# Attention and expert layers on one core: keys loaded by head pairs, and the last tile scaled in two halves

## The chip, the cores and the metric

The kernel runs on one core of a Trainium2 chip. Its engines are TensorE (PE in the rows; PEld is its weight load), VectorE (DVE), ScalarE (ACT), GpSimd (POOL) and SyncE (SP), which here issues most transfers between HBM and SBUF (on-chip memory). Matrix products go to PSUM. The metric is the device time of one execution in microseconds (us), as the median of several runs.

## The reference

Attention in a window, then a layer of eight experts of which each token takes one, all in float32:

```python
batch, n_heads, seq, head_dim = (8, 8, 576, 64)
scores = scale * np.matmul(q, k.transpose(0, 1, 3, 2))
mask = (rel >= 0) & (rel < window)                      # window = 128
scores = np.where(mask, scores + bias[None], -1000000000.0)
attn = np.exp(scores - np.max(scores, axis=-1, keepdims=True))
attn = attn / (np.sum(attn, axis=-1, keepdims=True) + 1e-09)
x = np.matmul(attn, v)          # as (B*S, H*D) = (4608, 512)

logits = x @ w_gate             # eight experts
expert_idx = np.argmax(logits, axis=1)
# gate_w: the chosen expert's softmax value
h = np.maximum(xe @ w1[e], 0.0) # 512 -> 1024, for the tokens of expert e
out[mask] = gate_w[mask, None] * (h @ w2[e])   # 1024 -> 512
```

## The kernel before

**Attention in chunks.** 36 chunks of 128 queries each, all eight heads (four head pairs; a pair's two heads lie in the two halves of the 128 partitions). A batch has 576 queries: four chunks m = 0 to 3, and a rest of 64. The rests of an even and the following odd batch share one *tail* chunk, which stands between the two: batch 0 has chunks 0 to 3, chunk 4 is the tail of batches 0 and 1, batch 1 has chunks 5 to 8, and so on. So an odd batch is first used in a tail chunk (13 for batch 3, 22 for batch 5, 31 for batch 7), an even one in its chunk m = 0 (9 for batch 2, 18 for batch 4, 27 for batch 6). A query sees the 128 keys up to its own, so chunk m reads columns 128(m - 1) to 128(m + 1) of the keys, and a tail chunk columns 384 to 576.

**Order of the work.** The table `WHEN` places each operation of a chunk in the order of program, in units of a chunk: S0 and S1 (`scores`, line 161) compute the scores of head pairs 0 and 1, and of 2 and 3; then come the maximum, the exponentials, the transposes, the products with the values and so on, up to four chunks later. Each engine runs its own instructions in the order in which the program has them, and waits at semaphores for the others. In `scores`, matmuls of a bias (line 173) come first, then 16 products of queries and keys (line 182) in four rounds of four: the first pair of the two for subblocks 0 to 3 and both heads, then the second pair. In the trace each of the 16 has two rows. In a tail chunk subblocks 0 and 1 are of the even batch, 2 and 3 of the odd one, so that the odd batch's second pair is in the last quarter.

**Loads of keys.** `batch[b]` is a tile `k_sb` of 128 partitions x 4 pairs x 576 columns, two of them in turn. `load_k(b, i)` (line 59) loads piece i. For batches 0 and 1 calls stand in the opening; for batches 2 to 7 a step (a quarter of a chunk) has them, counted from the batch's first chunk `ch` (line 273):

```python
ahead.setdefault(4 * ch + KA + KD * p, []).append((load_k, b, p))   # KA = -16, KD = 4
```

So pieces 0 to 3 are issued 16, 12, 8 and 4 steps before the batch's first chunk in the order of program. SP, which issues them, also has the queries, the values, the expert weights and the writes of finished rows in its queue, in the order of program. A piece is a range of columns of all four pairs, `KEYS = ((0, 128), (128, 256), (256, 384), (384, S))`; an odd batch begins with the last range.

**Expert layers.** From about 220 us on, TensorE runs eight experts one after another. In `layer2` (line 931) the last product of a tile (f == 7) is followed by a multiplication with the gate, from PSUM to SBUF: ScalarE has the even tiles, VectorE the odd ones (lines 944 to 947). Then GpSimd scatters the rows to `out` (`put`, line 926). The last expert has 462 places: four tiles, the last (t = 3) with 78 rows. A similar pair is in `narrow` (lines 919 to 922), where ScalarE scales one group of rows of a tile and VectorE the next.

Of the kernel before, what the change touches and what calls it, by code (L numbers as in the profile page):

```python
# [14 lines left out]
AF = mybir.ActivationFunctionType  # L15
ALU = mybir.AluOpType
# [5 lines left out]
N, DM, E, F = B * S, H * D, 8, 1024  # L22
# [14 lines left out]
def attention(ctx, tc, st, qT, qE, kT, v, c1, cb, iw, load_c2, logits, chunk_done, chunks, begun):  # L37
    nc = tc.nc
# [12 lines left out]
    batch = {}  # L51
# [7 lines left out]
    def load_k(b, i, gate=False):  # L59
        if b not in batch:  # L60
            batch[b] = qkv.tile([128, NP, S], F32, name="k_sb", bufs=2)
        c, d = KEYS[(i - b % 2) % 4]
        x = batch[b][:, :, c:d]
        if gate:
            hold(x[:, 0, 0:1])
        nc.sync.dma_start(out=x, in_=kT[b][:, :, c:d])

    def hold(x):
        keep(tc, nc.vector.memset(x, 0.0))
# [68 lines left out]
    for p in (0, 2):  # L138
        nc.vector.tensor_scalar(out=q0[:, p:p + 2], in0=q0[:, p:p + 2], scalar1=0.125, scalar2=1.0, op0=ALU.mult, op1=ALU.mult)
    load_q(0, 1)  # L140
    load_k(0, 1)
    load_c2(0, 128)

# [4 lines left out]
    for n, (f, b, m) in dict(q2=(load_q, 0, 2), k2=(load_k, 0, 2), q3=(load_q, 0, 3), k3=(load_k, 0, 3), q4=(load_q, 0, 4),  # L148
                             r4=(load_q, 1, 4), k4=(load_k, 1, 0), r0=(load_q, 1, 0), k5=(load_k, 1, 1), r1=(load_q, 1, 1),
                             k6=(load_k, 1, 2), k7=(load_k, 1, 3)).items():  # L150
        loads[n] = lambda gate, f=f, b=b, m=m: f(b, m, gate)
# [244 lines left out]
PROF = tuple(-(-c // 128) for c in CAPS)  # L396
# [17 lines left out]
KEYS = ((0, 128), (128, 256), (256, 384), (384, S))  # L414
# [384 lines left out]
def moe_static(ctx, tc, st, w12, out):  # L799
    nc = tc.nc  # L800
# [14 lines left out]
    ys = {}  # L815
# [7 lines left out]
    def column(p, t):  # L823
        return st["idx"][:, t:t + 1] if p == 0 else st["pidx"][:, p * TT + t:p * TT + t + 1]
# [101 lines left out]
    def put(**kw):  # L926
        ins = nc.gpsimd.indirect_dma_start(**kw).ins  # L927
        tc.declare_no_dep(ins, group="rows", reason="every token is in one slot: the rows are distinct")
        tc.add_to_no_dep_group("rows", ins)

    def layer2(p, f, wh, wl, hh, hl, tiles=None):
        for t in range(PROF[p] - (p in NARROW)) if tiles is None else tiles:
            if f == 0:
                ys[t] = ps_y[t > 1].tile([128, DM], F32, name=f"y{t}_ps")
            n = min(128, CAPS[p] - 128 * t)
            tl = slice(128 * t, 128 * t + n)
            gh, gl = h0[f] if p == 0 and t < 2 else (hh, hl)
            for k, (a, b) in enumerate(((gh, wh), (gh, wl), (gl, wh))):
                nc.tensor.matmul(out=ys[t][0:n], lhsT=a[:, tl], rhs=b[:, 512:1024],  # L939
                                 start=(f == 0 and k == 0), stop=(f == 7 and k == 2))  # L940
            if f == 7:
                y = yp.tile([128, DM], F32, name="y")
                gt = xs[p][2]
                if t % 2 == 0:
                    nc.scalar.activation(out=y[0:n], in_=ys[t][0:n], func=AF.Copy, scale=gt[0:n, t:t + 1])  # L945
                else:
                    nc.vector.tensor_scalar(out=y[0:n], in0=ys[t][0:n], scalar1=gt[0:n, t:t + 1], scalar2=None, op0=ALU.mult)
                put(
                    out=out[:, :], out_offset=bass.IndirectOffsetOnAxis(ap=column(p, t)[0:n], axis=0),
                    in_=y[0:n], in_offset=None, bounds_check=N - 1, oob_is_err=False,  # L950
                )
# [5 lines left out]
    for f in range(NE):  # L957
        layer2(0, f, *w0[f], None, None, (0, 1))
        if f == 1:
            order = order_experts(tc, st, bank())  # L960
            next(order)
        if f in PF:
            prep(0, 2 + PF.index(f))
        if f in OS:
            next(order, None)
# [4 lines left out]
    for p in range(E):  # L970
        if p in NARROW:
            load_narrow(p, 0)
        for f in range(8):
            cur = layer1(p, f)
            if p + 1 < E:
                t = f - (p + 1 >= BY_PARTS)
                if 0 <= t < PROF[p + 1]:
                    gather(p + 1, t, cur[2] if p + 1 >= BY_PARTS else None)
                for t in range(PROF[p + 1]):
                    if f == min(t + (PP if p else PP0), 7):  # L980
                        prep(p + 1, t)
            if 8 * p + f > 8 * E - LAST:
                held.append(pend)
            elif pend is not None:
                layer2(*pend, whole if pend[0] == 0 and pend[1] < NE else None)
                if pend[0] in NARROW and pend[1] in (3, 7):
                    narrow(pend[0], pend[1] // 4)
            if (p, f) == (1, 0):
                overflow_table(tc, st)
            if (p, f) == (E - 1, 1):  # L990
                keep(tc, nc.gpsimd.drain())
            pend = (p, f) + cur
    held.append(pend)
    for t in range(PROF[-1]):
        for x in held:
            layer2(*x, (t,))
# [344 lines left out]
```

## Time and profile before

| | |
|---|---|
| median of 3 runs | 644.63 us (644.35 to 645.72) |
| the profiled execution | 642.3 us, of which the span is 640.6 us |
| TensorE busy | 626.6 us, 98% of the span |
| its weight loads (beside it) | 536.9 us, 84% |
| VectorE / ScalarE / GpSimd busy | 380.9 / 316.4 / 294.5 us: 59%, 49%, 46% |
| mean granted TensorE clock | 0.996 of 2.4 GHz |
| transfers | 97.44 MB, mean 152 GB/s |

The span reaches from the first to the last instruction of the profiled execution; all times of rows count from its start. Busy shares are averages over stages: attention lies between 0 and some 220 us, the experts behind it. Matmuls are pipelined, so two that follow each other overlap in the rows. The time of a transfer "to landing" counts from its issue by SP to the last update of its semaphore.

### The profile page before, as it was taken

How to read it: one execution, taken by the hardware profiler on the slowest of the kernel's cores; microseconds unless marked ns; L12 is line 12 of the kernel's file. 1: busy time of each engine (PE TensorE's matmuls, PEld its weight loads, DVE VectorE, ACT ScalarE, POOL GpSimd, SP SyncE). 2: the span in 40 equal slices, each digit the busy share in tenths (PEclk: the TensorE clock that was granted, in tenths of full speed). 3: DMA queues.
4: the chain of work that ended last, by engine and by line, in shares of the span. 5: the costliest groups of instructions: out<-in, count | busy, mean ns of one | idle time of the engine just before them, and what ended most of it. 6: DMA issues, size and time to landing. Idle time of an engine off the chain costs nothing.

```text
span 640.6 us, 17972 instructions
## 1 busy us (share of the span) xinstructions
PE 626.6 (98%) x7125; PEld 536.9 (84%) x7125; DVE 380.9 (59%) x949; ACT 316.4 (49%) x963; POOL 294.5 (46%) x405
## 2 busy tenths in 40 slices
PE   7999999999999999999999999999999999999995
PEld 4788888878887888988988898898898888888884
DVE  4568877969888785536553654555456355455411
ACT  6878889888878314524342334334233333434311
POOL 2644656858646050067227607733750750670202
PEclk9999999999999999999999999999999999999998
DMA  8775996786743162374535325433442632543101
GB/s 249 237 228 156 293 277 192 216 289 190 220 143 86 51 189 81 144 251 112 185 123 165 106 77 184 117 100 134 143 118 86 196 113 70 183 128 125 65 1 61
DMA packets 60072, 97.44 MB, mean 152 GB/s; under 512 B 12293, under 2 KB 30597, under 8 KB 59986
## 3 DMA queue, kind: packets, MB, share of 16 engines
q1 hardware_dynamic: 51362, 76.25, 38.7%
q0 software_dynamic: 8336, 19.76, 10.7%
q8 instruction: 57, 0.93, 0.6%
q10 hardware_dynamic: 288, 0.26, 0.1%
q14 instruction: 29, 0.24, 0.1%
HBM read 77.27 MB, written 18.98 MB: 150 GB/s over the span
## 4 chain that ended last, share of the span: by engine, by line
PE 80%; issue 9%; POOL 4%; DVE 3%; ACT 1%; DMA 1%; SPq 0%; POOLq 0%; ACTq 0%; DVEq 0%
PE y_ps L939 25%; PE l_ps L734 24%; PE b_ps L240 9%; PE s_ps L182 5%; PE b_ps L209 5%; PE r_ps L248 5%; PE s_ps L173 2%; POOL xg L714 2%; PE s_ps L734 1%; POOL out L927 1%; ACT pe L201 1%; DMA c_sb<-c 1%; DVE nmax L195 1%; DVE s_ps L192 1%; PE x_ps L695 1%
## 5 line engine op out<-in xcount | busy, mean ns | idle before, releaser
L737 ACT ACTIVATE hh<-l_ps 128x320 fp32r<-128x320 f32 (+5 forms) x104 | 46.3, 446 | 199.2 <-PE l_ps L734 195.8
L741 DVE SCALAR_TENSOR_TENSOR hl<-l_ps,hh 128x320 fp32r<-128x320 f32 (+5 forms) x104 | 52.1, 501 | 147.0 <-ACT hh L737 146.8
L714 POOL DMA_INDIRECT xg<-xd,od_idx x112 | 116.5, 1040 | 34.5 <-issue 33.1
L201 ACT ACTIVATE pe<-s_ps,nmax 128x128 f32<-128x128 f32 x288 | 106.3, 388 | 31.7 <-DVE nmax L195 22.8
L939 PE MATMUL y_ps<-wh,hh 128*128 128x512 f32 (+5 forms) x280 | 110.3, 394 | 0.0
L939 PE MATMUL y_ps<-wl,hh 128*128 128x512 f32 (+5 forms) x280 | 109.8, 392 | 0.0
L939 PE MATMUL y_ps<-wh,hl 128*128 128x512 f32 (+5 forms) x280 | 109.7, 392 | 0.0
L927 POOL DMA_INDIRECT out<-y,od_pidx x33 | 34.6, 1049 | 150.0 <-ACT y L945 143.7
L224 POOL TENSOR_SCALAR_AFFINE_SELECT pT<-pT 128x512 f32<-128x512 f32 x112 | 71.4, 645 | 60.0 <-ACT pT L304 56.9
L1032 DVE TENSOR_TENSOR wl<-w_raw,wh 128x512 fp32r<-128x512 f32 x114 | 73.8, 689 | 33.2 <-ACT wh L1028 32.9
L734 PE MATMUL l_ps<-xh,wh 128*128 128x320 f32 (+8 forms) x416 | 81.2, 317 | 0.0
L734 PE MATMUL l_ps<-xl,wh 128*128 128x320 f32 (+8 forms) x416 | 80.6, 316 | 0.0
L734 PE MATMUL l_ps<-xh,wl 128*128 128x320 f32 (+8 forms) x416 | 80.4, 315 | 0.0
L734 PEld LDWEIGHTS l_ps<-xh,wh 128*128 128x128 f32 x416 | 67.8, 188 | 8.3 <-issue 1.2
L734 PEld LDWEIGHTS l_ps<-xl,wh 128*128 128x128 f32 x416 | 66.0, 188 | 2.0
L734 PEld LDWEIGHTS l_ps<-xh,wl 128*128 128x128 f32 x416 | 65.9, 188 | 2.0
L240 PE MATMUL b_ps<-pT,v_sb 128*64 128x128 f32 (+2 forms) x1152 | 66.3, 265 | 0.6 <-issue 0.6
L240 PEld LDWEIGHTS b_ps<-pT,v_sb 128*64 128x64 f32 (+1 forms) x1152 | 57.1, 136 | 9.7 <-issue 5.2
L201 ACT ACTIVATION_READ_ACCUMULATOR pe<-s_ps,nmax 128x1 f32 x288 | 64.5, 224 | 0.0
L939 PEld LDWEIGHTS y_ps<-wh,hl 128*128 128x128 f32 (+5 forms) x280 | 51.3, 183 | 13.2
L1028 ACT CAST wh<-w_raw 128x1024 fp32r<-128x1024 f32 x57 | 59.5, 1043 | 5.9 <-DMA w_raw<-w 5.9
L939 PEld LDWEIGHTS y_ps<-wl,hh 128*128 128x128 f32 (+5 forms) x280 | 51.3, 183 | 10.8
(216 smaller groups left out, 914.9 us busy)
## 6 DMA issues: line engine op xcount, KB each, us to landing
w_raw<-w SPq DMA_DIRECT2D x56, 512.0 KB, 3.6
xd<-x_sb SPq DMA_DIRECT2D x32, 258.0 KB, 4.1
v_sb<-v SPq DMA_DIRECT2D x32, 256.0 KB, 4.7
q_sb<-qT SPq DMA_DIRECT2D x31, 256.0 KB, 4.1
k_sb<-kT SPq DMA_DIRECT2D x23, 256.0 KB, 5.1
w_raw<-w SPq DMA_DIRECT2D x16, 256.0 KB, 4.5
k_sb<-kT SPq DMA_DIRECT2D x8, 384.0 KB, 4.5
w_n<-w SPq DMA_DIRECT2D x3, 1024.0 KB, 6.9
```

What stands on the lines that cost most here:

```text
L182: nc.tensor.matmul(out=s_ps[rows(u), c, n, x0:x1], lhsT=blocks["q", b, m][h, 2 * g + n, rows(u % 2 if tail else u)], rhs=batch[b][h, 2 * g ...
L201: nc.scalar.activation(out=pe[:, h, :], in_=s_ps[:, c, n, lo:lo + 128], func=AF.Exp, bias=nmax[:, 2 * c + n:2 * c + n + 1], scale=1.0, acc ...
L224: nc.gpsimd.affine_select(out=part(cut(kb)), in_=part(cut(1)), pattern=pat(sign), base=0, channel_multiplier=-sign, compare_op=op, fill=0.0)
L240: nc.tensor.matmul(out=x_ps[64 * c:64 * c + 64, p, q], lhsT=blocks["v", b, m - 1 + kb][0:kk, D * h:D * h + D], rhs=pT[0:kk, kb, h, q], sta ...
L714: ins = tc.nc.gpsimd.indirect_dma_start(out=g[:, s], out_offset=None, in_=parts, in_offset=bass.IndirectOffsetOnAxis(ap=idx[:, s], axis=0),)
L734: nc.tensor.matmul(out=ps, lhsT=a[:, 128 * d:128 * d + 128], rhs=b[:, d], start=(k == 0), stop=(k == 11))
L737: nc.scalar.activation(out=hh, in_=ps, func=AF.Relu)
L741: nc.vector.scalar_tensor_tensor(out=hl, in0=ps, scalar=0.0, in1=hh.bitcast(F32), op0=ALU.max, op1=ALU.subtract)
L927: ins = nc.gpsimd.indirect_dma_start(**kw).ins
L939: nc.tensor.matmul(out=ys[t][0:n], lhsT=a[:, tl], rhs=b[:, 512:1024], start=(f == 0 and k == 0), stop=(f == 7 and k == 2))
L1028: keep(tc, nc.scalar.copy(out=wh, in_=raw))
L1032: keep(tc, eng.tensor_tensor(out=wl[:, sl], in0=raw[:, sl], in1=wh.bitcast(F32)[:, sl], op=ALU.subtract))
```

## The change

For batches 2 to 7 a piece of keys is one head pair with all its 576 columns, in the order 0 to 3 for odd and even batches. The calls stay where they are. In the last tile of the last expert ScalarE scales the first 256 columns and VectorE the other 256; the other tiles are scaled as before.

```diff
     def load_k(b, i, gate=False):
         if b not in batch:
             batch[b] = qkv.tile([128, NP, S], F32, name="k_sb", bufs=2)
-        c, d = KEYS[(i - b % 2) % 4]
+        if b > 1:
+            nc.sync.dma_start(out=batch[b][:, i], in_=kT[b][:, i])
+            return
+        c, d = KEYS[(i - b) % 4]
         x = batch[b][:, :, c:d]
...
                 gt = xs[p][2]
-                if t % 2 == 0:
-                    nc.scalar.activation(out=y[0:n], in_=ys[t][0:n], func=AF.Copy, scale=gt[0:n, t:t + 1])
-                else:
-                    nc.vector.tensor_scalar(out=y[0:n], in0=ys[t][0:n], scalar1=gt[0:n, t:t + 1], scalar2=None, op0=ALU.mult)
+                half = DM // 2 if (p, t) == (E - 1, PROF[-1] - 1) else DM * (t % 2 == 0)
+                if half:
+                    nc.scalar.activation(out=y[0:n, 0:half], in_=ys[t][0:n, 0:half], func=AF.Copy, scale=gt[0:n, t:t + 1])
+                if half < DM:
+                    nc.vector.tensor_scalar(out=y[0:n, half:], in0=ys[t][0:n, half:], scalar1=gt[0:n, t:t + 1], scalar2=None, op0=ALU.mult)
                 put(
```

Line numbers move: the new loads stand in line 63, the score products in 185 (182 before), the scalings in 949 and 951 (945 and 947).

**SP, the third and fourth load of batch 5.** Its queue in chunks 20 and 21, with what each row waits for (DMAHW is a transfer's semaphore); `xd` are written rows, `w_raw` expert weights. Before:

```order
L66 DMA k_sb<-kT 128x4x128 [waits DMAHW1_49]
L1274 DMA xd<-x_sb_116 128x516 [waits DMAHW2_49,DVE_49]
L1017 DMA w_raw<-w 128x512 [waits DMAHW3_49,Activation_49,Pool_49]
L89 DMA v_sb<-v 128x512 [waits DMAHW4_49]
L80 DMA q_sb<-qT 128x512 [waits DMAHW5_49,PE_49,Pool_49]
L66 DMA k_sb<-kT 128x4x128 [waits DMAHW6_49]
```

Now:

```order
L63 DMA k_sb<-kT 128x576 [waits DMAHW1_49]
L1278 DMA xd<-x_sb_116 128x516 [waits DMAHW2_49,DVE_49]
L1021 DMA w_raw<-w 128x512 [waits DMAHW3_49,Activation_49,Pool_49]
L92 DMA v_sb<-v 128x512 [waits DMAHW4_49]
L83 DMA q_sb<-qT 128x512 [waits DMAHW5_49,PE_49,Pool_49]
L63 DMA k_sb<-kT 128x576 [waits DMAHW6_49]
```

The places and the waits are the same; only what the two loads bring has changed.

**TensorE, S1 of tail chunk 22, where batch 5 is first used.** `pT` and `v_sb` are operands of a product of an earlier chunk. Before:

```order
L173 LDWEIGHTS cb_sb
L173 MATMUL s_ps<-cb_sb 32x2x160
L182 MATMUL s_ps<-k_sb,q_sb 32x160 x16
L240 MATMUL b_ps<-pT,v_sb 64x128 [waits Activation_49,Pool_49]
L240 MATMUL b_ps<-pT,v_sb 64x128
L240 MATMUL b_ps<-pT,v_sb 64x128 [waits DMAHW3_49,Pool_49]
```

Now:

```order
L176 LDWEIGHTS cb_sb
L176 MATMUL s_ps<-cb_sb 32x2x160
L185 MATMUL s_ps<-k_sb,q_sb 32x160 x4
L185 MATMUL s_ps<-k_sb,q_sb 32x160 [waits DMAHW1_49]
L185 MATMUL s_ps<-k_sb,q_sb 32x160 x7
L185 MATMUL s_ps<-k_sb,q_sb 32x160 [waits DMAHW6_49]
L185 MATMUL s_ps<-k_sb,q_sb 32x160 x3
L243 MATMUL b_ps<-pT,v_sb 64x128 [waits Activation_49,Pool_49]
```

The 16 products waited for no load of their own before; now the fifth waits for pair 2 and the thirteenth for pair 3, the two loads shown above.

**VectorE, its last rows of the last expert.** `y` is the scaled tile. Before:

```order
L741 SCALAR_TENSOR_TENSOR hl_5127<-l_ps,hh_5126 128x462 [waits Activation_49]
L741 SCALAR_TENSOR_TENSOR hl_5129<-l_ps,hh_5128 128x462 [waits Activation_49]
L741 SCALAR_TENSOR_TENSOR hl_5125<-l_ps,hh_5124 128x462 [waits Activation_49]
L947 TENSOR_SCALAR y<-y_ps,gt 128x512 [waits DMASW3_49,PE_49]
L947 TENSOR_SCALAR y<-y_ps,gt 78x512 [waits DMASW5_49,PE_49]
```

Now:

```order
L744 SCALAR_TENSOR_TENSOR hl_5127<-l_ps,hh_5126 128x462 [waits Activation_49]
L744 SCALAR_TENSOR_TENSOR hl_5129<-l_ps,hh_5128 128x462 [waits Activation_49]
L744 SCALAR_TENSOR_TENSOR hl_5125<-l_ps,hh_5124 128x462 [waits Activation_49]
L951 TENSOR_SCALAR y<-y_ps,gt 128x512 [waits DMASW3_49,PE_49]
L951 TENSOR_SCALAR y<-y_ps,gt 78x256 [waits DMASW5_49,Activation_49]
```

The last row has half the columns, and it waits for ScalarE where it waited for TensorE.

## Rows read from the trace of the kernel before

**Rows 1.** The page's part 1: busy us (share of the span) xinstructions

```profile
PE 626.6 (98%) x7125; PEld 536.9 (84%) x7125; DVE 380.9 (59%) x949; ACT 316.4 (49%) x963; POOL 294.5 (46%) x405
```

**Rows 2.** Windows: us, busy of each engine (instructions), granted clock, DMA share, GB/s

```profile
30.00:125.00 95.00, 94.38 (x2237) 79.03 (x2243) 75.09 (x188) 80.15 (x335) 55.37 (x96) 1.00 0.77 225
125.00:220.00 95.00, 93.07 (x1982) 78.99 (x1967) 76.33 (x218) 70.77 (x290) 52.80 (x86) 1.00 0.59 177
```

**Rows 3.** Waits of PE, 30 to 230 us: total us, times, longest

```profile
PE s_ps L173 <- ACT pe L201: 0.7, 2, 0.4
PE s_ps L182 <- issue: 0.6, 1, 0.6
```

**Rows 4.** Transfers, 30 to 190 us: count, KB each, median us to landing

```profile
v_sb<-v SPq DMA_DIRECT2D x26, 256.0 KB, 4.9
q_sb<-qT SPq DMA_DIRECT2D x23, 256.0 KB, 4.1
k_sb<-kT SPq DMA_DIRECT2D x19, 256.0 KB, 5.2
```

**Rows 5.** Line 66 (loads of keys) over the span

```profile
DMA to landing us min/median/max: 3.3/4.7/7.6
```

**Rows 6.** SP's timeline, fourth loads of batches 3, 5, 6, 7: start, duration

```profile
71.36 0.55 SPq L66 DMA_DIRECT2D k_sb<-kT  x1
...
121.34 0.59 SPq L66 DMA_DIRECT2D k_sb<-kT  x1
...
147.99 0.55 SPq L66 DMA_DIRECT2D k_sb<-kT  x1
...
171.93 0.55 SPq L66 DMA_DIRECT2D k_sb<-kT  x1
```

**Rows 7.** Landings: keys of 71.36, 121.34, 147.99, 167.03; values of 120.34

```profile
DMA to landing us min/median/max: 3.9/3.9/3.9
...
DMA to landing us min/median/max: 7.6/7.6/7.6
...
DMA to landing us min/median/max: 3.8/3.8/3.8
...
DMA to landing us min/median/max: 4.7/4.7/4.7
...
v_sb<-v SPq DMA_DIRECT2D x1, 256.0 KB, 5.4
```

**Rows 8.** PE's timeline, S1 of chunks 13, 22, 27, 31: start, duration

```profile
74.65 0.73 PE L182 MATMUL s_ps<-k_sb,q_sb 64*32 64x160 f32 x32
...
124.93 0.73 PE L182 MATMUL s_ps<-k_sb,q_sb 64*32 64x160 f32 x32
...
154.44 0.64 PE L182 MATMUL s_ps<-k_sb,q_sb 64*32 64x32 f32 x32
...
176.18 0.73 PE L182 MATMUL s_ps<-k_sb,q_sb 64*32 64x160 f32 x32
```

**Rows 9.** Tile q_sb, 30 to 190 us, its products: ns min/median/max

```profile
L182 PE MATMUL s_ps<-k_sb,q_sb x1824: 186/296/321, 30.8 to 187.8; 64*32 64x160 f32 x141, 64*32 64x32 f32 x15, 64*32 64x96 f32 x11, 64*32 64x128 f32 x10
```

**Rows 10.** Timeline, end of the last expert, PE, DVE and ACT

```profile
633.39 0.40 PE L939 MATMUL y_ps<-wh,hl 128*78 128x512 f32 x1
...
633.83 0.75 DVE L947 TENSOR_SCALAR y<-y_ps,gt 78x512 f32<-78x512 f32 x1 [2.02 <-PE y_ps L939]
...
632.43 0.69 ACT L945 ACTIVATE y<-y_ps,gt 128x512 f32<-128x512 f32 x1 [1.85 <-PE y_ps L939]
```

**Rows 11.** Timeline, lines 920 and 922, ACT and DVE

```profile
274.44 0.46 ACT L920 ACTIVATE y<-y_ps,g_n 36x256 f32<-36x256 f32 x1
...
274.94 0.49 DVE L922 TENSOR_SCALAR y<-y_ps,g_n 36x256 f32<-36x256 f32 x1 [1.70 <-ACT y L920]
```

**Rows 12.** Windows at the end, columns as in rows 2

```profile
630.00:634.00 4.00, 3.79 (x17) 2.50 (x15) 0.93 (x2) 1.27 (x2) 2.53 (x3) 1.00 0.24 95
...
636.00:640.60 4.60, 0.00 (x0) 0.00 (x0) 0.00 (x0) 0.00 (x0) 0.00 (x0) 0.50 0.14 42
```


## Prediction

> **What bounds the kernel now.** I read the page first. TensorE is busy for 98% of the span [rows 1]; of the other engines none has over 59% (the table above). Then the windows, since attention (to about 220 us) and the expert layers have different limits: from 30 to 220 us, where the changed loads lie, TensorE works 187.45 of 190 us, at the granted clock 1.00 [rows 2]. Third, whom TensorE waited for there: 0.7 us on ScalarE in two waits, the rest "issue"; no row names a load [rows 3]. So TensorE is the bound, the keys are never late, and anything that makes TensorE wait is added to the end almost one to one. What it can give back behind 125 us is its idle time there, 95.00 - 93.07 = 1.93 us [rows 2].
>
> **The change, the keys.** For six batches (2 to 7), four loads of columns (128x4x128 or 128x4x192) become four loads of one head pair (128x576), at the same places of SP's queue: 24 loads, the same bytes, longer runs. Before, a chunk needed two of the four pieces and the other pieces only chunks later. Now a batch's first chunk needs all four: S0 reads pairs 0 and 1, S1 pairs 2 and 3. The pairs are issued 16, 12, 8 and 4 steps ahead, a chunk being four steps; the last has one chunk, and less where SP lags behind. The matmul that now waits stands in TensorE's own queue, and everything behind it waits with it.
>
> The pieces of before went out at the same places, so their issue times can be held against the first use of pair 3. The last load of batches 3, 5 and 7 left SP at 71.36, 121.34 and 171.93 [rows 6]. The S1 scores that will need it, in the tail chunks 13, 22 and 31, start at 74.65, 124.93 and 176.18 and take 0.73 [rows 8]; pair 3 of the odd batch is in the last of four equal rounds, and a matmul of these takes 0.30 [rows 9], so that round starts (0.73 - 0.30) = 0.43 in. From issue to need there are 3.7, 4.0 and 4.7 us. For the even batches the lead is longer; the shortest of the three is batch 6: issued 147.99 [rows 6], needed in a chunk that starts 154.44 [rows 8], 6.4 us against a landing of 3.8 [rows 7]. I cost these three at nothing, and pair 2 as well: it goes out a chunk earlier.
>
> Landing is the unknown. Key loads took 3.3 at least, 4.7 in the middle, 7.6 at most [rows 5]. The three loads in question, as pieces of 256 KB:
> - Batch 3: 3.9 [rows 7], so 0.2 late. Bounds: 0 (3.3) and 3.9 (7.6).
> - Batch 5: 7.6 [rows 7], the slowest of all, because four large transfers go out just ahead of it; the values issued 1.0 us earlier took 5.4 [rows 7]. Late by 7.6 - 4.0 = 3.6 at the same landing, by 1.4 at 5.4, by nothing at 3.3. I take the middle of the two nearest rows, 6.5: 2.5 us.
> - Batch 7: its landing isn't told; the key load before it took 4.7 [rows 7], so 0.0. Bounds 0 and 2.9.
>
> Stall together: 0.2 + 2.5 + 0.0 = 2.7 us (0 to 10.4).
>
> Do longer runs land sooner? A transfer of 288 KB is 1/8 more than 256 KB. Against it, queries and values of 256 KB, whose runs are 2,048 bytes, land in 4.1 and 4.9 us where key pieces take 5.2 [rows 4], 0.3 to 1.1 less; but they leave at other moments of the queue, so I leave the landings as they are and keep 1.1 for the range. The Trainium skill (DMA: Bandwidth & Descriptors, Specifications) asks for runs of at least 512 B for line rate. The old runs of 128 floats are exactly that; by this rule the longer runs buy no rate, the extra 32 KB costs a little, and the stall stays at 2.7 or grows. By the rows on queries and values batch 5's stall would be 1.4 instead of 2.5. No row isolates the run's length.
>
> **The change, the last tile.** Before: the last matmul runs 633.39 to 633.79, VectorE starts at 633.83 and takes 0.75 for 78x512 [rows 10], until 634.58; the scatter follows. Now ScalarE takes 256 columns and VectorE 256. In the new order VectorE's half waits for ScalarE (and not for TensorE), so it comes behind ScalarE's half. The trace has such a pair: ScalarE 0.46 for 36x256 at 274.44, then VectorE 0.49 at 274.94, 0.04 behind the other's end [rows 11]. 633.83 + 0.46 + 0.04 + 0.49 = 634.82, 0.24 us later than before. ScalarE is free: its previous tile ends at 632.43 + 0.69 = 633.12 [rows 10]. If the halves ran side by side it would be 0.75 - 0.49 = 0.26 less; those are the bounds.
>
> The Trainium skill (PSUM — Partial Sum Buffer, PSUM bank collisions raise a hardware error) says that two engines must not touch one bank in the same 32 partitions at once, readers and disjoint columns included. A tile of 512 float columns fills a bank, so by that rule two halves by columns can never overlap; the pair above agrees with it.
>
> **Sum.** 2.7 + 0.24, and of TensorE's 1.93 us of idle time behind chunk 22 I let 0.3 be given back (the waits on other engines are small [rows 3]): +2.6 us. The profiled execution took 642.3 us (span 640.6), which would become 644.9; it is 2.3 below the median of the runs shown, so I add to the median: 644.63 + 2.6 = 647.2.
>
> **Rivals.**
> - Landings in time. The 24 loads make fewer, longer runs and the queue ahead of batch 5's last pair drains sooner: landing 4.1, as the queries [rows 4], is 0.1 late; the other two 0.4 and 0. With the tail, and 0.3 given back, +0.4: 645.0. For it: the median of key loads is 4.7. Against: the DMA engines are loaded at 77% from 30 to 125 us [rows 2], and this one load took 7.6.
> - Faster. The freed transfer time removes idle time that TensorE has: two waits of 0.6 for "issue" stand among its waits (one shown in [rows 3]), and all its idle time from 30 to 220 us is 0.62 + 1.93 = 2.55 [rows 2]. Only if no pair is late and more than 1.55 of these 2.55 goes (1.3 and the tail's 0.24) does it decide; at 1.8 the time is 644.63 - 1.8 + 0.24 = 643.1. Against: none of it is a wait for a load.
> - The clock falls. A stall of about 3 us is longer than any idle time of TensorE in attention; the granted clock is 1.00 (2.4 GHz) up to 634 us and 0.50 (1.2 GHz) from 636 us, when the engine had nothing more to do [rows 12]. If the stall in chunk 22 lets it fall and it stays down for as long as is seen there, 4.6 us, half of that is lost: 647.2 + 2.3 = 649.5. The Trainium skill (TensorE: Matmul & The Clock Gate, Part 1) has the same two levels and says that activity lifts the lower one; the end of this trace agrees.
>
> **How the numbers follow.** The forecast (late pairs, 647.2) has a chance of 0.52, in time 0.28, the clock 0.10, faster 0.10. A measurement of this kernel can tell about 0.2%, 1.3 us. So slower 0.62, same 0.28, faster 0.10. The forecast's own range is 645.9 to 648.6 (batch 5 late by 1.4 to 3.6, the others by up to 0.4 more). The range reaches from the case in time and a part of the faster one to a part of the clock's: 643.9 to 650.0.
>
> **What would show it.** In the changed trace: a wait of TensorE on the scores' line for the keys' load, above all in chunk 22 near 125 us (2.5 us), hardly any in chunks 13 and 31, none in the even batches; VectorE's last row 78x256 starting 0.04 behind ScalarE's; the landing of 128x576 loads. If no row of TensorE's waits names the keys, the first rival holds. If stalls appear but the end moves less, idle time behind them was larger than the 0.3 that I gave. Stalls of several us in chunks 13 or 31 would make it slower than the range.

## The result, and the profile after

The changed kernel takes 648.86 us (median of 8 runs, 647.59 to 651.01); the kernel before, beside it on the same chip, 645.67 (8 runs, 644.29 to 646.84). The ratio is 1.0056, with a 95% interval of 1.0037 to 1.0074: 3.6 us slower (2.4 to 4.8); the two medians lie 3.2 us apart. The forecast was +2.6 us, from 644.63 to 647.2.

The profiled execution of the changed kernel took 651.01 us (span 649.2), the longest of its eight; one trace is one draw, and the experiments add others. First its engines, as in [rows 1]:

```profile
PE 629.9 (97%) x7125; PEld 538.0 (83%) x7125; DVE 379.4 (58%) x949; ACT 317.3 (49%) x964; POOL 295.7 (46%) x405
```

TensorE has the same 7125 products and is busy 3.3 us longer. The windows of [rows 2] (busy of PE, PEld, DVE, ACT, POOL; then granted clock, DMA share, GB/s):

```profile
30.00:125.00 95.00, 92.65 (x2209) 77.34 (x2208) 72.53 (x186) 79.06 (x331) 53.72 (x93) 1.00 0.72 220
125.00:220.00 95.00, 90.68 (x1958) 76.03 (x1943) 72.23 (x192) 71.39 (x289) 55.60 (x89) 0.98 0.60 176
```

TensorE's idle time from 30 to 220 us rose from 2.55 to 2.35 + 4.32 = 6.67, and in the second stretch the mean granted clock is no longer 1.00. Whom it waited for from 30 to 230 us (total, times, longest), where [rows 3] named no load:

```profile
PE s_ps L185 <- DMA k_sb<-kT: 5.0, 2, 3.3
PE s_ps L176 <- ACT pe L204: 0.6, 2, 0.4
PE s_ps L176 <- DVE p L541: 0.6, 1, 0.6
```

Two waits for keys, 5.0 us. PE's timeline shows where they stand: S1 of the chunks of [rows 8] (start, duration; in brackets the wait before the row and what ended it).

```profile
75.03 0.71 PE L185 MATMUL s_ps<-k_sb,q_sb 64*32 64x160 f32 x24
77.44 0.48 PE L185 MATMUL s_ps<-k_sb,q_sb 64*32 64x160 f32 x8 [1.70 <-DMA k_sb<-kT]
77.84 0.55 PE L243 MATMUL b_ps<-pT,v_sb 128*64 128x128 f32 x6
...
127.34 0.71 PE L185 MATMUL s_ps<-k_sb,q_sb 64*32 64x160 f32 x24
131.39 0.76 PE L185 MATMUL s_ps<-k_sb,q_sb 64*32 64x160 f32 x8 [3.33 <-DMA k_sb<-kT]
132.08 3.15 PE L243 MATMUL b_ps<-pT,v_sb 128*64 128x128 f32 x32
...
160.76 0.64 PE L185 MATMUL s_ps<-k_sb,q_sb 64*32 64x32 f32 x32
...
182.50 0.73 PE L185 MATMUL s_ps<-k_sb,q_sb 64*32 64x160 f32 x32
```

Chunks 13 and 22, the tail chunks of batches 3 and 5, run 24 of their 32 records and then wait: the last quarter holds the odd batch's second pair. Chunk 31 (batch 7) and the even batches (chunk 27) run as before. A wait costs more than its row says, since the row counts from the end of the 24th record (0.71 us after S1's start), and without a wait the 25th would have started before that: in chunk 13 the 25th record comes 77.44 - 75.03 = 2.41 us after S1's start, where 0.73 - 0.30 = 0.43 was the plan, so it is 2.0 late for a wait of 1.70; in chunk 22, 131.39 - 127.34 - 0.43 = 3.6 for 3.33. I use this lateness below, since the forecast counted it so. What comes next is a little later still. The row behind S1 in the kernel before, chunk 22:

```profile
125.58 1.97 PE L240 MATMUL b_ps<-pT,v_sb 128*64 128x128 f32 x32
```

It starts 125.58 - 124.93 = 0.65 us after S1 did; now, in chunk 13, 77.84 - 75.03 = 2.81, so the work behind the wait is 2.16 late. In this and the later traces, in the ten waits of S1 behind which its last quarter ran at the full clock (0.48 us), that is 0.46 to 0.47 us more than the wait's row.

SP's issues of the four loads of [rows 6], and what the chain that ended last now has for two of them (start, duration):

```profile
70.89 1.01 SPq L63 DMA_DIRECT2D k_sb<-kT  x1
...
123.76 0.42 SPq L63 DMA_DIRECT2D k_sb<-kT  x1
...
154.09 0.48 SPq L63 DMA_DIRECT2D k_sb<-kT  x1
...
178.24 0.43 SPq L63 DMA_DIRECT2D k_sb<-kT  x1
```

```profile
70.89 6.50 DMA k_sb<-kT
...
123.76 7.59 DMA k_sb<-kT
```

This trace has no landings of its own; in the chain, issue to release took 6.50 and 7.59 us where [rows 7] had 3.9 and 7.6. (Where a later trace has both, they agree within 0.1.)

Behind chunk 22's wait something came on top. Windows of 2 us, the granted clock in the third column from the right:

```profile
126.00:128.00 2.00, 2.00 (x43) 1.54 (x42) 1.97 (x7) 1.32 (x7) 1.93 (x4) 1.00 0.75 240
128.00:130.00 2.00, 0.06 (x4) 0.00 (x0) 0.25 (x1) 2.00 (x9) 2.00 (x3) 1.00 1.04 395
130.00:132.00 2.00, 0.61 (x8) 0.20 (x8) 0.00 (x0) 0.05 (x1) 1.40 (x4) 0.78 1.08 233
132.00:134.00 2.00, 2.00 (x22) 1.92 (x20) 1.12 (x2) 0.47 (x3) 0.00 (x0) 0.50 1.04 354
134.00:136.00 2.00, 2.00 (x68) 1.79 (x64) 0.20 (x1) 1.06 (x4) 0.00 (x0) 0.87 1.05 388
136.00:138.00 2.00, 2.00 (x27) 1.80 (x16) 0.93 (x3) 1.63 (x8) 0.40 (x1) 1.00 0.28 100
```

TensorE stood still, then worked at 0.50 (1.2 GHz), then at 1.00 again. The price is in PE's timeline: from the fourth quarter of chunk 22's S1 to S0 of chunk 23 it took 135.63 - 131.39 = 4.24 us; a trace of the same loads in which the clock stayed at 1.00 has 130.77 - 127.99 = 2.78 (the first experiment): 1.5 us for the lower clock.

The end, which answers to [rows 10]:

```profile
642.35 0.40 PE L942 MATMUL y_ps<-wh,hl 128*78 128x512 f32 x1
...
642.78 0.47 ACT L949 ACTIVATE y<-y_ps,gt 78x256 f32<-78x256 f32 x1 [0.70 <-PE y_ps L942]
643.29 0.48 DVE L951 TENSOR_SCALAR y<-y_ps,gt 78x256 f32<-78x256 f32 x1 [2.52 <-ACT y L949]
```

The two halves run one behind the other, VectorE 0.04 us after ScalarE. From the end of the last product to the end of the scaling: 643.77 - 642.75 = 1.02 us, where it was 634.58 - 633.79 = 0.79.

### The profile page after: what moved, and what is told of

Same layout as the page of the kernel before. It is cut to its first block, busy times and chain, and to the rows that moved or that the text cites. A ratio compares the mean times of both kernels' runs of the same rounds, so it can differ in the third digit from the quotient of the medians.

```text
span 649.2 us, 17954 instructions
## 1 busy us (share of the span) xinstructions
PE 629.9 (97%) x7125; PEld 538.0 (83%) x7125; DVE 379.4 (58%) x949; ACT 317.3 (49%) x964; POOL 295.7 (46%) x405
## 4 chain that ended last, share of the span: by engine, by line
PE 80%; issue 8%; DMA 4%; DVE 2%; POOL 2%; ACT 2%; POOLq 0%; SPq 0%; ACTq 0%; DVEq 0%
PE y_ps L942 27%; PE l_ps L737 26%; PE b_ps L243 8%; PE s_ps L185 5%; PE b_ps L212 5%; PE r_ps L251 4%; DMA k_sb<-kT 2%; PE s_ps L176 2%; ACT pe L204 2%; PE s_ps L737 1%; POOL out L930 1%; DMA q_sb<-qE 1%; DVE nmax L198 1%; POOL xg L717 1%; PE x_ps L698 1%
## 5 line engine op out<-in xcount | busy, mean ns | idle before, releaser
L942 PEld LDWEIGHTS y_ps<-wh,hh 128*128 128x128 f32 (+5 forms) x280 | 51.4, 184 | 10.2 <-ACT hh L740 0.6
```

## The experiments

The theory: the last pair of an odd batch, issued one chunk ahead, lands after its first use. The rivals: the shape of the loads costs time everywhere; the tail does it; the clock does it. A ratio is that to the kernel before on the same chip; it isn't the quotient of the two medians, from which it differs by up to 0.3%.

**Each part alone.** Head pairs without the new tail; then the new tail without head pairs.

```diff
-        c, d = KEYS[(i - b % 2) % 4]
+        if b > 1:
+            nc.sync.dma_start(out=batch[b][:, i], in_=kT[b][:, i])
+            return
+        c, d = KEYS[(i - b % 2) % 4]
```

> The keys of batches 2 to 7 come by head pairs, the last tile is scaled by VectorE alone as before. Lateness (my theory): TensorE waits for the last pair in chunk 13 (about 1.7 us) and chunk 22 (about 3.3 us), as in the changed kernel's trace, and the median is 2.5 to 4 us over that of before (ratio 1.004 to 1.006). Rival, the split tile costs a good part of it: the median is within 1.5 us of before.

```diff
+                half = DM // 2 if (p, t) == (E - 1, PROF[-1] - 1) else DM * (t % 2 == 0)
+                if half:
+                    nc.scalar.activation(out=y[0:n, 0:half], in_=ys[t][0:n, 0:half], func=AF.Copy, scale=gt[0:n, t:t + 1])
+                if half < DM:
+                    nc.vector.tensor_scalar(out=y[0:n, half:], in0=ys[t][0:n, half:], scalar1=gt[0:n, t:t + 1], scalar2=None, op0=ALU.mult)
```

> Only the last tile is scaled in two halves; keys by columns as before. Theory: VectorE's half starts some 0.04 us behind the end of ScalarE's and ends 0.24 us later than the one instruction did, which the medians can't resolve (ratio 0.998 to 1.002). Rival, the halves overlap: VectorE starts with ScalarE and the tile is done 0.25 us sooner. Rival, the tail costs a good part of the 3 us: ratio over 1.002.

Measured: head pairs alone 649.05 against 646.80, ratio 1.0062 (1.0039 to 1.0085); the tail alone 646.34, ratio 1.0002 (0.9984 to 1.0020). The keys are the whole effect that can be measured; by the medians they cost 2.3 us, a little under the 2.5 to 4 expected, by the ratio 4.0. In the trace of the tail alone VectorE's half starts 0.04 us behind ScalarE's, as expected. The trace with head pairs alone has both waits, in chunk 22 with 0.88 us far from the 3.3 expected, and the clock stays at 1.00 behind it. PE's timeline:

```profile
74.34 0.71 PE L185 MATMUL s_ps<-k_sb,q_sb 64*32 64x160 f32 x24
76.79 0.48 PE L185 MATMUL s_ps<-k_sb,q_sb 64*32 64x160 f32 x8 [1.74 <-DMA k_sb<-kT]
...
126.40 0.71 PE L185 MATMUL s_ps<-k_sb,q_sb 64*32 64x160 f32 x24
127.99 0.48 PE L185 MATMUL s_ps<-k_sb,q_sb 64*32 64x160 f32 x8 [0.88 <-DMA k_sb<-kT]
...
130.77 0.47 PE L185 MATMUL s_ps<-k_sb,q_sb 64*32 64x32 f32 x26
```

**Head pairs, all loads earlier.** Two steps between a batch's loads instead of four, so the last goes out 10 steps ahead; old tail. Beside it, later, columns at these same places.

```diff
-KD = 4
+KD = 2
```

> Head pairs as in the change, but the four loads are issued 16, 14, 12 and 10 steps ahead of the batch's first chunk instead of 16, 12, 8 and 4; last tile as before. Lateness: no wait of TensorE for keys above 0.2 us, and the median is back at that of before (ratio 0.998 to 1.002). Rival, it is the transfers' form (one long run of 2,304 bytes a partition, 288 KB) that costs: ratio stays at 1.004 or more. Rival, longer runs are worth something once they are not late: ratio under 0.998.

> Columns as before in all batches, but with 2 steps instead of 4 between a batch's loads (16, 14, 12 and 10 steps ahead). It stands beside the kernel with head pairs at these same places, which measured 1.0003. Theory (nothing is late in either, and the length of the runs brings nothing): ratio 1.000, within 0.002 of the head pairs. Rival (long runs give time back, which the earlier places cost elsewhere): columns at these places are slower than head pairs at them, 1.002 to 1.004.

Measured: head pairs 646.42, ratio 1.0003 (0.9989 to 1.0017); columns 643.67 on a chip where the kernel before took 643.86, ratio 1.0012 (0.9993 to 1.0031). With time enough, head pairs cost nothing that these intervals can tell, and gain nothing over columns. The waits of PE with head pairs, 30 to 230 us, name no load:

```profile
PE b_ps L243 <- ACT pT L307: 0.9, 1, 0.9
PE s_ps L185 <- issue: 0.6, 1, 0.6
PE b_ps L243 <- issue: 0.5, 2, 0.3
```

**Even or odd batches alone.** The condition for head pairs; b % 2 == 1 in the second run.

```diff
-        if b > 1:
+        if b > 1 and b % 2 == 0:
```

> Head pairs for batches 2, 4 and 6 alone; the odd batches keep columns, the last tile is as before. Lateness as I worked it out by batch: the even batches have 6.4 us or more from issue to need, so no wait for keys over 0.2 us, ratio 0.998 to 1.002. Rival, each batch's loads cost their share: half of the loss, ratio 1.002 to 1.003.

> Head pairs for batches 3, 5 and 7 alone; batches 2, 4 and 6 keep columns, and the last tile is scaled as before. Theory (the last pair of an odd batch comes too late for the tail chunk that uses it first): the whole loss of the six batches together, ratio to before 1.004 to 1.006, waits of TensorE for the keys of 1 to 2 us in chunk 13 and 1 to 3.5 us in chunk 22, none in chunk 31. Rival (longer runs or the different order of rows in transfers slow everything that shares the DMA engines): half of the loss, 1.002 to 1.003, spread over waits that no row names, as half of the loads are changed. If the even batches bear a part of it after all: 1.002 to 1.004.

Measured: even batches 646.72 against 646.80, ratio 1.0019 (1.0001 to 1.0038), with no wait for keys among TensorE's waits; odd batches 646.00 against 643.86, ratio 1.0037 (1.0018 to 1.0056), with waits in chunks 13 and 22. The odd batches alone are slower and hold every wait that the trace shows, but two expectations were missed: the ratio is under the 1.004 to 1.006 of the whole loss and within the 1.002 to 1.004 that I gave for a part borne by the even batches, and chunk 13's wait is 0.59 where 1 to 2 us were expected. For the even ones the medians are equal but the interval just leaves out 1: a share of theirs of up to 0.4% isn't excluded, though no wait shows one. In the trace of the odd batches the clock again fell behind chunk 22 (timeline, then windows):

```profile
76.17 0.48 PE L185 MATMUL s_ps<-k_sb,q_sb 64*32 64x160 f32 x8 [0.59 <-DMA k_sb<-kT]
...
128.75 0.58 PE L185 MATMUL s_ps<-k_sb,q_sb 64*32 64x160 f32 x8 [2.19 <-DMA k_sb<-kT]
```

```profile
128.00:130.00 2.00, 1.25 (x16) 0.90 (x18) 0.52 (x2) 0.51 (x1) 1.83 (x4) 0.75 1.08 258
130.00:132.00 2.00, 2.00 (x22) 2.00 (x20) 0.60 (x1) 0.81 (x4) 0.00 (x0) 0.50 1.03 320
```

**Lateness without head pairs.** Columns only, turned by one place, so that the piece which a batch needs first goes out last.

```diff
-        c, d = KEYS[(i - b % 2) % 4]
+        c, d = KEYS[(i - b % 2 + (b > 1)) % 4]
```

> No head pairs at all: batches 2 to 7 come by columns as before, but turned by one place, so that the piece which the first chunk needs goes out last, four steps ahead of it. Theory (what counts is the time from the last needed load's issue to its use, not the shape of the load): waits of TensorE for the keys in the S0 scores of tail chunks 13, 22 and 31, where 0.6 to 1.6 us are left against a landing of 3.8 to 7.6: 2 to 3 us, 3 to 7 us and 2 to 3 us, some of it beside a lower granted clock behind the longest one; together 8 to 13 us, ratio 1.012 to 1.022; in the even batches 0 to 1 us. Rival (the shape of the transfers makes the loss): ratio 1.000, since each transfer is one that the kernel before has too.

Measured: 660.59 against 643.86, ratio 1.0269 (1.0241 to 1.0298), 17.3 us. The shape of the loads is that of the kernel before, so lateness alone makes TensorE wait. The loss is above what I expected: the waits in S0 of chunks 13 and 31, 4.0 and 3.4 us, were above the expected 2 to 3, that of chunk 22, 6.0, within 3 to 7, and the clock fell behind all three, not one. PE's timeline and windows behind each:

```profile
77.44 1.10 PE L182 MATMUL s_ps<-k_sb,q_sb 64*32 64x160 f32 x24 [4.00 <-DMA k_sb<-kT]
...
135.40 1.29 PE L182 MATMUL s_ps<-k_sb,q_sb 64*32 64x160 f32 x24 [6.00 <-DMA k_sb<-kT]
...
191.50 1.29 PE L182 MATMUL s_ps<-k_sb,q_sb 64*32 64x160 f32 x24 [3.41 <-DMA k_sb<-kT]
```

```profile
78.00:82.00 4.00, 4.00 (x45) 3.36 (x40) 1.82 (x5) 1.45 (x6) 1.27 (x2) 0.61 0.43 94
...
136.00:140.00 4.00, 4.00 (x48) 3.34 (x44) 1.73 (x5) 1.36 (x6) 1.52 (x2) 0.61 0.20 49
...
190.00:194.00 4.00, 2.50 (x30) 1.98 (x31) 1.05 (x3) 0.08 (x1) 0.00 (x0) 0.54 0.57 187
194.00:198.00 4.00, 4.00 (x61) 3.24 (x61) 1.08 (x5) 2.51 (x10) 1.91 (x4) 0.60 0.00 0
```

**Only the last pair earlier, by two steps.** Head pairs as in the first experiment, and:

```diff
-                ahead.setdefault(4 * ch + KA + KD * p, []).append((load_k, b, p))
+                ahead.setdefault(4 * ch + KA + KD * p - 2 * (p == 3), []).append((load_k, b, p))
```

> Head pairs for six batches, as in the change, but the last pair of each batch goes out 6 steps ahead of its first chunk instead of 4, about 1.8 to 2.5 us sooner; the other three stay, and the last tile is scaled as before. Theory (lateness of the last pair): chunk 13's wait of 1.7 us goes to 0 and chunk 22's of 1 to 3.3 us to 0 to 1; no window of a lower granted clock; ratio 1.000 to 1.002. Rival (a load of a head pair lands later whatever its place): waits of over 1 us remain in both chunks, ratio 1.003 to 1.006.

Measured: 644.42 against 643.86, ratio 1.0004 (0.9987 to 1.0020). Two steps for one load in four bring the loss back, as far as the interval can tell. Chunk 13 now runs through; chunk 22 is at the edge (its S1 takes 1.09 us where 0.73 is undisturbed):

```profile
74.69 0.73 PE L185 MATMUL s_ps<-k_sb,q_sb 64*32 64x160 f32 x32
...
125.46 1.09 PE L185 MATMUL s_ps<-k_sb,q_sb 64*32 64x160 f32 x32
```

**Traces again.** One landing per load was all that the prediction had. The kernel before, the six batches' head pairs (tail as before) twice more, and the odd batches' once more, one execution each: 644.63, 646.24, 647.11 and 645.13 us, beside 643.93 for another of the kernel before, too few for ratios.

> The kernel before once more, for a second trace of its loads. In the first trace the last load of batch 3 landed after 3.9 us and that of batch 5 after 7.6. Theory (a landing at one place of the queue varies from execution to execution by 1 to 3 us, so one trace's row is a poor estimate of it): batch 3's lands after 4.5 to 6.5 or batch 5's after 5 to 6.5 here; the two are not both within 0.3 of the first trace. Rival (the place decides, and head pairs land later than columns at it): 3.9 and 7.6 again, within 0.3.

> Head pairs for six batches, tail as before: the kernel of the first experiment again. Theory (landings vary): the waits in chunks 13 and 22, 1.7 and 0.9 us there, differ by over 0.5 us in at least one of the two; if chunk 22's is above 2 us, a window of a lower granted clock follows it, if it is under 1.5, none. Rival (the place decides): both within 0.3 of the first trace.

> Head pairs for batches 3, 5 and 7 alone, again. Theory (landings vary): waits in chunks 13 and 22, 0.6 and 2.2 us before, each between 0 and 3.5, at least one of them changed by over 0.5; a lower granted clock only behind a wait above 2 us. Rival (the place decides): 0.6 and 2.2 again, within 0.3.

> Head pairs for six batches, tail as before, a third trace. Theory (landings vary): together with the two others the waits in chunk 13 spread over at least 0.5 us and those in chunk 22 over at least 1 us. Rival (the place decides): within 0.3 of each other.

Measured (us; landing of the batch's last load, from its record or from the chain; the wait; clock fallen: whether the windows behind chunk 22 show 0.50):

| kernel | batch 3 lands | wait, chunk 13 | batch 5 lands | wait, chunk 22 | clock fallen |
|---|---|---|---|---|---|
| before | 3.9 | none | 7.6 | none | no |
| before, again | 4.7 | none | 5.8 | none | no |
| odd batches | 4.9 | 0.59 | 6.2 | 2.19 | yes |
| odd batches, again | 5.7 | 1.49 | 6.6 | 1.84 | no |
| six batches | 6.1 | 1.74 | 5.6 | 0.88 | no |
| six batches, again | 6.3 | 1.88 | 6.4 | 2.04 | no |
| six batches, third | 6.5 | 1.89 | 6.6 | 2.37 | yes |
| the change | 6.5 | 1.70 | 7.6 | 3.33 | yes |

Most of what I expected held. Batch 5's landing varies between executions (5.6 to 7.6, alike for columns and pairs), and chunk 22's wait with it, by 1.5 us in three traces of one kernel. Two expectations failed: no lower clock follows the wait of 2.04, and chunk 13's wait spread by only 0.2 us, not 0.5. Batch 3's landing varies less, 3.9 and 4.7 for columns, 6.1 to 6.5 for six batches of pairs. With pairs in the odd batches alone it is 4.9 and 5.7, so the pairs of the even ones may add to chunk 13's wait; these few traces don't show that they do. Size alone doesn't decide: in the columns turned by one place, batch 3's last load has 384 KB and landed after 5.6. Nor is it the key load alone that lands later. Transfers issued from 69.9 to 71.3 us (count, KB, us to landing), in the second trace of the kernel before, then in that of the six batches' pairs:

```profile
q_sb<-qT SPq DMA_DIRECT2D x1, 256.0 KB, 4.3
w_n<-w SPq DMA_DIRECT2D x1, 256.0 KB, 4.9
k_sb<-kT SPq DMA_DIRECT2D x1, 256.0 KB, 4.7
```

```profile
k_sb<-kT SPq DMA_DIRECT2D x1, 288.0 KB, 6.3
q_sb<-qT SPq DMA_DIRECT2D x1, 256.0 KB, 5.3
w_n<-w SPq DMA_DIRECT2D x1, 256.0 KB, 6.4
```

All three land 1.0 to 1.6 us later. Why (more bytes in the key loads, 288 KB where 256 was, issues that come sooner as SP spends about 0.43 instead of 0.58 us on a key load, or something else) wasn't taken apart and stays open.

## Why the prediction was right

**The mechanism** held: a wait on the scores' line for the keys, in the last quarter of S1, in the tail chunks of odd batches, none in chunk 31 and none in the even batches. Taking the lateness away (1.0003, 1.0004) takes the loss away; adding lateness without head pairs (1.0269) makes it. One sign of it failed: chunk 13 was to show hardly any wait, and it has one of 1.7 to 1.9 us in each trace with six batches of pairs.

**The stall's size** was the sum of three terms, 2.7 us. Lateness (25th record, as above) in the four traces with six batches of pairs (the change, then the three with the old tail):
- Batch 3, forecast 0.2: measured 2.0, 2.0, 2.2, 2.2. This is the term that was mis-sized. I took its landing from one row of the kernel before (3.9 in [rows 7]) and left it as it was; with pairs it is 6.1 to 6.5. SP issued it a little sooner against its use (75.03 + 0.43 - 70.89 = 4.6 us of lead, not 3.7), which took 0.9 of the 2.6 back.
- Batch 5, forecast 2.5: measured 3.6, 1.2, 2.3, 2.7, a mean of 2.4. The landing taken, 6.5, between two rows, is about the mean of the four (6.6). That is luck in part: single traces gave 5.6 to 7.6. The reason given for the 7.6, four large transfers just ahead, isn't shown either: the same queue brought this load in 5.8 in the second trace of the kernel before.
- Batch 7, forecast 0: none.

Together about 4.5 us, not 2.7; for the work behind the waits, 0.18 later in each chunk, 4.9.

**Given back** were not 0.3 but some 2 us: 4.9, the tail's 0.24 and 0.7 for the lower clock (1.5 in two traces of four), less the measured 3.6, leave 2.2 (1.0 to 3.4 by the interval). So the stall was not added "almost one to one", as the prediction has it. TensorE's idle time agrees. In the second trace of the kernel before the two windows are

```profile
30.00:125.00 95.00, 93.72 (x2216) 78.31 (x2215) 76.33 (x186) 79.91 (x335) 54.65 (x95) 1.00 0.77 220
125.00:220.00 95.00, 91.35 (x1969) 77.38 (x1969) 75.15 (x205) 70.71 (x285) 53.59 (x86) 1.00 0.61 177
```

with 1.28 + 3.65 = 4.9 us of it, where the first had 2.55: one trace's idle time is one draw, too. In the seven traces of all runs without a wait for keys there it is 2.5 to 4.9 us, 3.7 on average. In the seven with one, less these waits, it is 1.6 to 2.3, 2.0 on average; the change has 6.67 - 5.03 = 1.64. Some 1.7 us of short idle times vanished beside the stalls.

So the stall was put 2.2 us too low, the clock's 0.7 was left out of the sum, and what is given back was put 1.9 too low: that +2.6 comes near +3.6 is errors of opposite sign in part. As a time, 648.86 lies within the range that was given (643.9 to 650.0) but above the forecast's own (645.9 to 648.6), since the kernel before took 1.0 us longer beside it than the 644.63 that I added to; as an increase, 3.6 lies within that range's 1.3 to 4.0.

**The clock** was a rival with 0.10 that would add 2.3 us. It doesn't take the theory's place but stands beside it, in a part of the executions: it fell in two of the four traces with six batches of pairs and in one of the two with three, so 0.10 was too little. Its price was 1.5 to 1.6 us in these three, not 2.3. How often it falls in the timed runs is open. The Trainium skill (TensorE: Matmul & The Clock Gate, Part 1) tells of the same two levels, the lower one after idleness; the windows above agree.

**The tail**, +0.24: measured 1.02 - 0.79 = 0.23, with VectorE 0.04 us behind ScalarE as in the pair of [rows 11]; alone it can't be told from nothing (1.0002).

**The longer runs** bring nothing that can be measured: 1.0003 with them and 1.0012 without at the same places, each against its own chip's kernel before. That is what the Trainium skill (DMA: Bandwidth & Descriptors, Specifications) leads to, which asks for 512 B, the length of the old runs.

Of the other rivals, landings in time (+0.4) and faster fell by the interval of the ratio. The changed kernel's profiled execution also lost 1.9 us behind attention, where the change has nothing but the tail: from the last product of queries and keys to the last of the expert layers it took 435.8 us, the kernel before 433.9. That isn't the change: four traces from one chip (each part alone, all loads earlier with head pairs, even batches), have 435.0 to 436.8, the tail alone 436.0, and the eight others, from two more chips, 433.6 to 434.7.

## What to carry to other kernels

How a load is cut decides when its first use has all of it: count the lead of the last piece that the first user needs, not that of the first, and give it more than the slowest landing seen at that place (here 7.6 us, against a lead of 4 to 5). A landing read from one trace is one draw, and with other loads in the queue it moves; two or three traces of the same kernel are worth more than a finer argument on one. A kernel whose bounding engine is 98% busy pays for most of a late load, here 3.6 of some 5.8 us (stall, lower clock and tail together), since short idle times vanish beside the stall; whether the clock falls behind it differs from execution to execution.

## What was not expected of the hardware

The granted clock went to 0.50 (1.2 GHz) behind waits of TensorE of 2.19, 2.37 and 3.33 us and behind the three of 3.41 to 6.00; behind those of 0.88, 1.84 and 2.04 in chunk 22, and of 0.59 to 1.89 in chunk 13, it stayed at 1.00. From 70 to 80 us, where batch 3's last load lands, the DMA share was 1.00 before and after the change, yet loads of 256 or 288 KB at this place landed after 3.9 to 6.5 us, and neighbours in the queue 1.0 to 1.6 us later together. The work behind a wait of TensorE in S1 came 0.46 us later than the wait's row says.
